# A list-ordered attention and mixer kernel: longer planned durations for batch 2's turned tiles, and a new order of its 1026 steps

## The chip, the cores and the metric

The kernel runs on one core of a Trainium2 chip. The metric is device time in microseconds (us); shown is the median of three runs of one build. Five engines work side by side, each through its own list of instructions in order: TensorE (PE, matmuls), VectorE (DVE), ScalarE (ACT), GpSimd (POOL) and SyncE (SP, which here only issues transfers). They wait for one another through semaphores.

## The reference

Batch 4, 8 heads, sequence 768, head size 48. The first half is a gated linear recurrence, the second an MLP mixer over its output:

```python
f = 1.0 / (1.0 + np.exp(-f_logit))
for t in range(S):
    state = f[:, :, t, :, None] * state + np.einsum('bhd,bhe->bhde', k[:, :, t], v[:, :, t])
    y[:, :, t] = np.einsum('bhd,bhde->bhe', q[:, :, t], state)
...
xt = x.transpose(0, 2, 1)
h = np.maximum(xt @ w_tok1, 0.0) @ w_tok2
u = x + h.transpose(0, 2, 1)
h2 = np.maximum(u @ w_ch1, 0.0) @ w_ch2
return (u + h2)
```

## The kernel before

The recurrence is computed in chunks. For each batch b the sequence is cut in three parts (P = 0, 1, 2) of two chunks each. Per part, ACT makes the logarithm of the gate (`gates`); DVE adds neighbouring steps (`two`); PE forms running sums; DVE and ACT make the gate factors (`first`, `GG`); DVE multiplies them into q and k (`qk`); these are turned so that head size lies on the partitions (`qT`, `kT`); PE forms the scores; DVE masks them (`AmT`, four tiles a part, with some of batch 0's masked by ACT and POOL together); PE forms the output (`within`, line 661, and the share of the state, `before`, line 655). Each state is copied to bf16 (`state_bd`, called sbd below). The mixer of a batch then runs tok1 (line 709), tok2 (725), the turn of u (`uT`), ch1 (784, in two halves th of the sequence, twelve columns cc each) and ch2 (803), and stores the result.

Batches 0 and 1 turn q, k and u with PE transposes that DVE or ACT copy out of PSUM. Batches 2 and 3 do it by transfers that SP issues: `dma_start_transpose` at line 531 (q into `qJ`, then rearranged into `qT` by POOL or ACT; k straight into `kT`) and at line 755 (u into `uT`).

No engine's list is in program order. `add` collects 1026 steps (ops); each knows what it needs and makes, on which engines it may run, and a cost. The tuple `ORDER` is a list written out by hand or by a search: an entry `code` stands for op `code // 4` on the engine number `code % 4` of those the op allows. `Plan.best` walks `ORDER`, gives each op a planned start (the latest of its inputs, its engine's last op and its PSUM bank), and emits the ops sorted by planned start. On any one engine that is the order of `ORDER` itself. The planned times decide two more things: which PSUM bank an op gets, and, before 25.5 us of planned time only, how many idle matmuls (line 852) fill PE's planned gaps.

A cost `("fix", own, till, wire, late)` says that the engine is taken for `own` ns, that the result is there after `till` ns, that the wires are taken for `wire` ns, and that `late` is added when the wires are busy. The planned gaps and banks come from these; the hardware waits for semaphores, not for planned times.

To read the ops that the text names: op 61 and 62 are the `qk` products of batch 0, part 0 (line 523); 64 and 66 its kT and qT (550); 86 and 88 the bf16 copies of its output (695); 92 is `first` of part 1 (499); 101 and 103 are kT and qT of part 1; 118 and 119 its second state copy (644); 143, 146 and 147 are DVE's masks of part 2 (624); 149 the state's decay of part 2 (633) and 150, 151 the copies of it; 121 and 153 are `within` of parts 1 and 2 (680); 14, 15 and 19 build the mask (408 to 412).

Of the kernel before, what the change touches and what calls it, by code (L numbers as in the profile page):

```python
# [255 lines left out]
def kernel(  # L256
# [45 lines left out]
    qk = [st([128, 2, 2, H, 64], BF16, f"qk{i}") for i in range(NQ)]  # L302
    qT = [st([128, HP, 128, 2], BF16, f"qT{i}") for i in range(NQ)]
    kT = [st([128, 2, HP, 128], BF16, f"kT{i}") for i in range(NQ)]
    qJ = [st([128, 2, HP, 128], BF16, f"qJ{i}") for i in range(2)]
# [580 lines left out]
```

## Time and profile before

| | |
|---|---|
| median of 3 runs | 166.11 us (165.8 to 166.11) |
| the profiled execution: its time / its span | 167.62 us / 165.9 us |
| granted TensorE clock, mean | 0.997 |
| busy: PE, DVE, ACT, POOL | 158.6, 128.8, 106.9, 61.7 us |
| instructions | 4990 |

The rows of the trace give a start, a length, an engine, the line of the kernel, the tile written and read, a count, and in square brackets how long the engine was idle before and what ended that. In the table of windows each row is a stretch of time and the busy time of each engine in it, with the count of instructions in parentheses. Rows of the chain of waits give start, length and what ran.

### The profile page before, as it was taken

The page shows a single profiled execution, that of the slowest core. Times are in us where ns is not written, and L with a number is a line of the kernel's source. Part 1 is how long each engine was busy: PE and PEld are TensorE (multiplying, and loading weights), DVE is VectorE, ACT ScalarE, POOL GpSimd, SP SyncE. Part 2 cuts the span into 40 slices and gives each one's busy share as a digit, 9 for nine tenths or more (in the row PEclk, how much of TensorE's full clock was granted, in tenths as well). Part 3 has the DMA queues.
Part 4 walks back from the last instruction along what each step waited for, and adds up shares of the span by engine and source line. Part 5 has one row for each costly group of instructions (what it writes and reads, how often), then busy time and mean ns, then how long its engine had stood idle before and what let it go on. Part 6 is the DMA issues. An engine that isn't in the chain of part 4 may idle for free.

```text
span 165.9 us, 4990 instructions
## 1 busy us (share of the span) xinstructions
PE 158.6 (96%) x2052; PEld 101.4 (61%) x2052; DVE 128.8 (78%) x284; ACT 106.9 (64%) x231; POOL 61.7 (37%) x86
## 2 busy tenths in 40 slices
PE   7889997999999999999999999999999999999992
PEld 3356765566667766666666765665666665656661
DVE  6748997589999999998999999988599526704331
ACT  3869784797899999999948966384811511623300
POOL 7961799964776820001914514200322020000000
PEclk9999999999999999999999999999999999999998
DMA  4999999999999999457699990991900030690506
GB/s 123 219 177 171 201 210 232 168 206 227 219 225 222 225 242 142 81 98 115 133 224 128 119 155 0 106 213 50 209 19 4 0 59 16 175 325 17 177 31 206
DMA packets 68183, 24.34 MB, mean 147 GB/s; under 512 B 60896, under 2 KB 67296, under 8 KB 68160
## 3 DMA queue, kind: packets, MB, share of 16 engines
q0 software_dynamic: 41856, 13.77, 68.2%
q1 hardware_dynamic: 25776, 10.06, 28.9%
q8 instruction: 16, 0.26, 0.7%
q10 hardware_dynamic: 528, 0.20, 0.4%
q14 instruction: 7, 0.06, 0.1%
HBM read 25.17 MB, written 4.72 MB: 180 GB/s over the span
## 4 chain that ended last, share of the span: by engine, by line
PE 82%; DMA 5%; ACT 4%; DVE 4%; issue 1%; POOL 1%; DVEq 0%; ACTq 0%; POOLq 0%
PE ps L803 28%; PE ps L784 28%; DMA qk_sb<-in_q_dram 5%; PE ps L709 5%; PE ps L725 4%; PE ps L665 3%; PE ps L581 3%; PE ps L657 2%; PE ps L546 2%; PE ps L599 2%; PE ps L766 1%; PE ps L481 1%; ACT state_bd L434 1%; ACT x_nat L434 1%; DVE qk L448 1%
## 5 line engine op out<-in xcount | busy, mean ns | idle before, releaser
L803 PE MATMUL ps<-w_ch,zT 128*128 128x384 bf16 (+2 forms) x300 | 54.0, 320 | 0.0
L784 PE MATMUL ps<-uT,w_ch 128*128 128x384 bf16 x288 | 51.6, 326 | 0.0
L784 PEld LDWEIGHTS <-w_ch 128*128 128x128 bf16 x288 | 27.8, 98 | 17.6
L803 PEld LDWEIGHTS <-zT 128*128 128x128 bf16 x300 | 27.9, 98 | 17.1
L443 ACT ACTIVATE zT<-ps 128x384 bf16<-128x384 f32 x57 | 25.1, 493 | 16.3 <-PE ps L784 16.1
L624 DVE TENSOR_TENSOR AmT<-ps,mask 128x512 bf16<-128x512 f32 x44 | 28.6, 685 | 1.5 <-PE ps L581 1.2
L445 DVE TENSOR_SCALAR zT<-ps 128x384 bf16<-128x384 f32 x39 | 20.6, 553 | 10.0 <-PE ps L784 8.9
L814 DVE TENSOR_TENSOR x_nat<-x_nat,ps 128x384 f32<-128x384 f32 (+2 forms) x25 | 13.1, 534 | 10.5 <-PE ps L803 10.5
L438 POOL CAST state_bd<-state 48x192 bf16<-48x192 f32 x15 | 5.7, 377 | 28.6 <-DVE state L641 25.8
L448 DVE TENSOR_TENSOR qk<-qk_sb,GG 128x768 bf16<-128x768 bf16 x24 | 12.9, 563 | 1.3 <-DMA qk_sb<-in_q_dram 1.3
L502 ACT ACTIVATE GG<-ps 128x384 bf16<-128x384 f32 x24 | 11.2, 485 | 3.5 <-DVE first L499 2.8
L357 POOL DMA_DIRECT2D v_sb<-in_v_dram x12 | 10.7, 894 | 6.3 <-DMA w_ch<-in_moe_w_ch_dram 3.7
L434 ACT ACTIVATE x_bf<-ps 128x384 bf16<-128x384 f32 x15 | 6.9, 483 | 8.5 <-PE ps L657 8.2
L519 ACT ACTIVATE GG<-first 128x384 bf16<-128x384 f32 x24 | 11.7, 517 | 0.2
L741 DVE TENSOR_TENSOR x_nat<-x_nat,ps 128x384 f32<-128x384 f32 x21 | 10.6, 549 | 1.4 <-PE ps L725 1.2
L357 POOL DMA_DIRECT2D qk_sb<-in_k_dram x12 | 10.9, 905 | 1.6 <-POOLq L870 0.8
L434 ACT ACTIVATE u_bf<-x_nat 128x384 bf16<-128x384 f32 x12 | 5.8, 518 | 8.6 <-DVE x_nat L741 8.6
L357 POOL DMA_DIRECT2D qk_sb<-in_q_dram x12 | 10.8, 898 | 0.5 <-DMA qk_sb<-in_q_dram 0.3
L852 PE MATMUL ps<-steady 128*128 128x512 f32 (+1 forms) x20 | 9.8, 610 | 1.0 <-DVE steady L372 1.0
L438 POOL COPY qT<-qJ 128x1024 bf16<-128x1024 bf16 x3 | 3.4, 1149 | 18.8 <-ACT zT L443 18.7
L709 PE MATMUL ps<-x_bf,w_tok 128*128 128x384 bf16 x48 | 10.4, 327 | 0.0
L434 ACT ACTIVATE x_nat<-ps 128x384 f32<-128x384 f32 x20 | 9.3, 492 | 0.1
(87 smaller groups left out, 231.3 us busy)
## 6 DMA issues: line engine op xcount, KB each, us to landing
out_dram<-x_nat SPq DMA_DIRECT2D x23, 192.0 KB, 2.3
f_sb<-in_f_logit_dram POOLq DMA_DIRECT2D x9, 384.0 KB, 8.9
qk_sb<-in_k_dram POOLq DMA_DIRECT2D x12, 192.0 KB, 8.8
qk_sb<-in_q_dram POOLq DMA_DIRECT2D x12, 192.0 KB, 9.0
v_sb<-in_v_dram POOLq DMA_DIRECT2D x12, 192.0 KB, 8.9
w_ch<-in_moe_w_ch_dram POOLq DMA_DIRECT2D x2, 576.0 KB, 9.0
w_ch<-in_moe_w_ch_dram POOLq DMA_DIRECT2D x1, 1152.0 KB, 10.6
f_sb<-in_f_logit_dram SPq DMA_DIRECT2D x2, 384.0 KB, 5.8
```

The costliest lines, as they stand in the source:

```text
L357: lambda eng=eng, into=held(dst[i], P), of=runs(src, b, P): eng.dma_start(out=into, in_=of),
L434: nc.scalar.activation(out_, in_, AF.Copy, bias=0.0, scale=1.0)
L443: nc.scalar.activation(out_, in_, AF.Relu, bias=0.0, scale=1.0)
L445: nc.vector.tensor_scalar(out_, in_, 0.0, None, ALU.max)
L448: (nc.vector if op.engine == DVE else nc.gpsimd).tensor_tensor(out_, a, b_, what)
L502: add(ACT, r, lambda n=n: nc.scalar.activation(GG[i][:, 1, n], sview(), AF.Exp, bias=0.0, scale=2.0 * n - 1.0), need=["tables"] if b == 0 ...
L519: add(ACT, r, lambda n=n: nc.scalar.activation(GG[i][:, 0, n], first[i], AF.Exp, bias=0.0, scale=2.0 * n - 1.0), need=[("first", i)] + ([" ...
L624: add(DVE, r, lambda into=into, made=made, m4=m4: nc.vector.tensor_tensor(into, made(), m4, ALU.mult), need=masks, make=[("AmT", i, js, pa ...
L709: add(PE, rank("tok1", rt), lambda rt=rt, kt=kt, pm=pm: nc.tensor.matmul(banks[pm.at][:, 0:DM], lhsT=w_tok1[:, kt, rt * 128:(rt + 1) * 128 ...
L784: nc.tensor.matmul(banks[pm.at][:, 0:384], lhsT=w[:, kt, c0:c0 + 128], rhs=uT[:, th, :, kt, :], start=(kt == 0), stop=(kt == 2))
L803: nc.tensor.matmul(banks[pm.at][:, 0:n1 - n0], lhsT=zT[:, kt, tt * 128:(tt + 1) * 128], rhs=w_ch2[:, kt, n0:n1], start=(kt == 0), stop=(kt ...
L814: add(DVE, rank("ch2", tt), lambda un=un, pm=pm, n=n1 - n0: nc.vector.tensor_tensor(un, un, banks[pm.at][:, 0:n], ALU.add), make=[("x_nat" ...
```

## The change

Two planned durations become functions of the batch, and the order is another one. No op is added or removed; what an op computes stays the same, but an op may run on another of the engines it allows.

```diff
-                    need=[("qk", s, 0), ("qk", s, 1)], make=[("qkT", s, 1) if n else ("qJ", i)], kind=("fix", 1350, 3400, 2000, 3500))
+                    need=[("qk", s, 0), ("qk", s, 1)], make=[("qkT", s, 1) if n else ("qJ", i)], kind=("fix", 1350, 4200 if b == 2 else 3800, 2000, 3500))
...
-                make=[("uT", 3 * th + j, d) for j in range(3) for d in range(3)], kind=("fix", 1350, 3400, 2000, 3500))
+                make=[("uT", 3 * th + j, d) for j in range(3) for d in range(3)], kind=("fix", 1350, 5200 if b == 2 else 3500, 2000, 3500))
```

Of `ORDER` nearly every line changes. Its first lines, which hold the part of batch 0 that the prediction walks through:

```diff
 ORDER = (
-    0, 4, 12, 16, 24, 28, 32, 8, 20, 188, 192, 196, 36, 40, 44, 76, 68, 48, 52, 60, 208, 356, 212, 220, 64, 224,
-    236, 240, 228, 360, 364, 368, 248, 244, 216, 376, 232, 372, 380, 388, 260, 80, 84, 265, 384, 200, 88, 296,
-    252, 92, 96, 56, 300, 256, 72, 309, 304, 396, 392, 204, 312, 268, 272, 504, 408, 400, 276, 288, 404, 316,
-    292, 280, 413, 508, 512, 320, 324, 100, 104, 108, 416, 420, 516, 448, 428, 452, 536, 532, 524, 520, 461,
-    457, 544, 540, 112, 116, 120, 284, 124, 128, 132, 432, 136, 328, 332, 340, 440, 344, 464, 336, 468, 348,
-    352, 444, 140, 476, 472, 556, 561, 528, 436, 424, 548, 552, 704, 592, 676, 708, 680, 564, 568, 596, 576,
-    572, 584, 588, 580, 480, 484, 488, 600, 604, 608, 612, 616, 493, 497, 144, 148, 152, 501, 621, 624, 156,
+    0, 4, 12, 16, 8, 20, 24, 28, 32, 188, 192, 196, 36, 40, 44, 56, 48, 52, 208, 212, 220, 64, 68, 356, 228,
+    224, 236, 240, 216, 232, 360, 364, 372, 244, 72, 248, 80, 88, 252, 260, 368, 256, 296, 300, 264, 305, 92,
+    96, 84, 200, 388, 384, 376, 308, 204, 380, 396, 392, 60, 312, 268, 272, 280, 316, 504, 76, 288, 276, 292,
+    400, 408, 508, 405, 320, 324, 413, 100, 104, 108, 512, 448, 416, 420, 516, 452, 461, 457, 524, 520, 540,
+    436, 424, 428, 532, 536, 440, 464, 544, 112, 116, 120, 124, 128, 132, 136, 140, 284, 144, 328, 332, 336,
+    556, 432, 444, 148, 348, 340, 468, 561, 528, 477, 548, 473, 552, 480, 484, 564, 568, 353, 576, 492, 497,
+    152, 580, 346, 156, 592, 704, 488, 676, 680, 708, 572, 588, 584, 608, 612, 596, 604, 600, 500, 616, 712,
...
```

Read as ops: 66 goes from ACT (265) to DVE (264), 101 from DVE (404) to ACT (405), 118 and 119 from ACT (472, 476) to DVE (473, 477), 86 from POOL (344) to DVE (346). On DVE op 92 (368) comes behind 61 and 62 (244, 248) instead of before them, 15 and 19 (60, 76) come later, and 149 (596) goes behind the masks 143, 147 and 146 (572, 588, 584). On POOL the weight loads and batch 1's first two loads (128 to 140) come before op 71 (284). SP's list begins as before with ops 2, 5 and 21; further on, both turns of u of batch 2 change places (707 before 706), and stores change places with transposes.

96 rows, old and new, of the table ORDER are left out of this document.

## The prediction

> **What bounds the kernel now.** I read the page first, then the windows of the trace, the chain of waits, and the timelines of PE and DVE over the first 35 us.
>
> ```profile
> span 165.9 us, 4990 instructions
> PE 158.6 (96%) x2052; PEld 101.4 (61%) x2052; DVE 128.8 (78%) x284; ACT 106.9 (64%) x231; POOL 61.7 (37%) x86
> ```
>
> The windows tell where PE's missing 4% lies:
>
> ```profile
> 25.00:30.00 5.00, 4.01 (x99) 2.67 (x92) 3.38 (x6) 2.39 (x6) 4.62 (x6) 1.00 1.39 218
> ...
> 35.00:40.00 5.00, 5.00 (x33) 2.98 (x32) 4.48 (x11) 4.67 (x13) 1.29 (x2) 1.00 1.45 234
> 40.00:60.00 20.00, 20.00 (x345) 13.62 (x344) 19.86 (x40) 18.53 (x41) 14.40 (x17) 1.00 1.80 219
> 60.00:80.00 20.00, 20.00 (x264) 13.08 (x262) 19.23 (x43) 19.65 (x44) 2.00 (x3) 1.00 0.87 123
> ```
>
> The first figure after the comma is PE; the windows from 80 to 160 us are as full. From 35 us on PE never stops, at a granted clock of 1.00. A busy PE could still be a slow one, so the chain of waits is asked for the pace:
>
> ```profile
> 34.12 2.93 PE ps L784 x18
> ```
>
> and, far behind,
>
> ```profile
> 107.38 3.90 PE ps L784 x24
> ```
>
> 2.93 / 18 and 3.90 / 24 both give 0.163 us a matmul of 384 columns, early and late alike. So after some 34 us the kernel is a fixed amount of PE work, and the end moves only by how early the head hands over to it, by stalls that a new order brings, and by the last store. (The Trainium skill, Perfetto Trace Analysis, section Identifying the Most-Contended Engine, calls matmul busy time a poor measure of what is left. By that rule a better order could still win behind a full PE; the one pace at both places speaks against it, and such a gain gets no term.)
>
> The head on PE:
>
> ```profile
> 25.96 0.57 PE L665 MATMUL ps<-v_sb,AmT 64*128 64x48 bf16 x31
> 27.52 0.18 PE L665 MATMUL ps<-v_sb,AmT 64*128 64x48 bf16 x1 [0.99 <-issue]
> ...
> 28.07 0.58 PE L665 MATMUL ps<-v_sb,AmT 64*128 64x48 bf16 x32
> ...
> 30.41 2.11 PE L725 MATMUL ps<-h1T,w_tok 128*128 128x384 bf16 x12
> ```
>
> Op 121 (`within` of part 1) runs 31 of its 32 matmuls, stands 0.99 us for nothing that the profile shows, and ends; op 153 (`within` of part 2) starts at 28.07, tok2 at 30.41. Had there been no stall, op 153 would have waited for DVE's last masks, which end at 24.92 + 1.89 = 26.81:
>
> ```profile
> 10.85 1.03 DVE L448 TENSOR_TENSOR qk<-qk_sb,GG 128x768 bf16<-128x768 bf16 x2 [1.32 <-DMA qk_sb<-in_q_dram]
> ...
> 24.92 1.89 DVE L624 TENSOR_TENSOR AmT<-ps,mask 128x512 bf16<-128x512 f32 x3
> ```
>
> From q's landing to the end of those masks, by one window:
>
> ```profile
> 10.85:26.81 15.96, 14.36 (x320) 10.23 (x321) 14.10 (x30) 11.92 (x25) 10.37 (x13) 1.00 1.53 198
> ```
>
> DVE, the third figure after the comma, is busy for 14.10 of 15.96 us and idle for 1.86. It is the head's engine.
>
> **The change, part by part.**
>
> *The longer durations.* A planned duration emits nothing. It moves a bank or the order, and idle matmuls only before 25.5 planned us, where batch 2 has no turned tile yet. Is there a wait on turned tiles that a later plan could save? Their landing times, of u:
>
> ```profile
> L755 SPq DMA_TRANSPOSE uT<-u_bf x4: 1281/1296/1627, 102.7 to 141.4; - x4
> ...
> DMA to landing us min/median/max: 3.2/3.2/4.5
> ```
>
> and of kT:
>
> ```profile
> DMA to landing us min/median/max: 3.0/3.5/6.8
> ```
>
> Some exceed the old 3.4 us, but PE is full where they are used: no wait, so 0 us. The cover was thin once: the first turn of u starts at 102.7 and, at the longest landing, is there at 107.2; ch1 of batch 2 starts at 107.38 in the chain above. In the new PE list nine groups of ch1 on the other half come first, 27 x 0.163 = 4.4 us, and cover the turn that is issued last. The price if a cover fails is what it lacks, at most 6.8 - 3.5 = 3.3 us for a landing at its worst; I take 0.
>
> *The order behind the head.* PE's work there is the same: 0 us unless a wait arises (rival three). Behind the last matmul the same two sums on DVE stand before the last store. On SP the stores of other rows before it are in another order, all ready before PE ends: 0, at most one store's issue, 0.4 us.
>
> *The head.* Before op 152, where part 2's output starts, PE's list holds the same 33 ops in both kernels, so what op 153 is shifted by, everything behind it is shifted by. On DVE, between 61 / 62 and the last of masks 143, 146, 147, ops come and go. By mean rows:
>
> ```profile
> L499 DVE TENSOR_TENSOR first<-ps,f_sb 128x384 f32<-128x384 f32 x12 | 6.6, 553 | 1.0 <-PE ps L486 1.0
> ...
> L436 DVE COPY kT<-ps 128x1024 bf16<-128x1024 bf16 x6 | 4.1, 686 | 0.1
> L436 DVE CAST x_bf<-ps 128x384 bf16<-128x384 f32 x6 | 3.3, 553 | 1.5 <-PE ps L657 1.4
> ...
> L436 DVE COPY qT<-ps 128x1024 bf16<-128x1024 bf16 x2 | 2.4, 1224 | 0.0
> ...
> L633 DVE TENSOR_TENSOR ps<-ps,glast 128x192 f32<-128x192 f32 x5 | 1.8, 363 | 1.3 <-PE ps L599 0.8 <-ACT glast L505 0.3 <-issue 0.2
> ...
> L436 DVE CAST state_bd<-ps 48x192 bf16<-48x192 f32 x3 | 1.1, 357 | 0.1
> ...
> L412 DVE COPY mask<-tri 64x64 bf16<-64x64 bf16 x2 | 0.7, 348 | 0.0
> L410 DVE TENSOR_TENSOR mask<-tri,ident 64x64 bf16<-64x64 bf16 x2 | 0.5, 228 | 0.0
> L408 DVE COPY mask<-tri 64x128 bf16<-64x128 bf16 x2 | 0.4, 216 | 0.0
> ```
>
> In come op 92, which ran while DVE waited for q and now stands behind it, 0.553; op 66, qT from ACT, 1.224; 118 and 119 from ACT, 2 x 0.357; 86 from POOL, 0.553 by its nearest row, which reads PSUM where op 86 reads SBUF; 19, 0.348; 15, 0.228: 3.62. Out go 101 (kT) 0.686, 149 0.363, 14 0.216: 1.27. The balance is 2.35. Rows of one engine overlap: three masks of 0.685 take 1.89, not 2.06, so 0.06 less each, 0.25 for the net four ops. That leaves 2.1 us more work on DVE.
>
> Against it stand the 1.86 us idle. In the new list DVE still waits for PE's turn of k in part 0 (about 0.1), for the first state product (0.2), and for part 2's turn of k (0.1): 0.45 with what lies between rows. So it eats 1.86 - 0.45 = 1.4, and the masks end 2.1 - 1.4 = 0.7 later, at 27.5. Bounds: 2.1 if it keeps every wait, 0 if the ops that ACT gave up shorten the remaining waits and DVE's queue packs closer. I take 0.7, from the waits whose causes stay. ACT's side: op 101 now stands ahead of 103 there, two copies of about 1 us in a row before part 1's scores, while DVE has part 0's three masks to do.
>
> In the old list PE still had op 122 and the state's share of op 153 to run after the masks (two times 0.17 us), in the new one op 122 lies earlier: -0.15. Against that, 149 and its copies 150, 151 now follow the masks:
>
> ```profile
> 26.06 0.67 ACT L434 ACTIVATE state_bd<-ps 48x192 bf16<-48x192 f32 x2 [0.47 <-PE ps L657]
> ```
>
> They take 0.36 + 0.67 us where op 153 itself gives 0.58 us of cover: `before(1)` of part 2 comes 0.45 late if nothing else is in the way, 0 if the copies of x_bf behind it set the pace. I take 0.25, the middle, for want of a row. Head: 0.7 - 0.15 + 0.25 = +0.8, against an old head without the stall, with bounds of -0.2 and +2.3.
>
> *The stall.* The profiled execution has 167.62 us with a span of 165.9; the median is 1.51 us lower, which leaves room for timed runs without the 0.99. I take the stall as the profiled execution's own. (The Trainium skill, Runtime: NRT & Kernel Launch, section Instruction fetch mechanics, has the refill of an engine's instructions mostly hidden; by that rule a stall without a releaser is no regular cost, and the sum stays. No row here shows a refill at 26.5 us.)
>
> **Sum.** Against the profiled execution: 167.62 - 0.99 + 0.8 = 167.4. For the median: 166.11 + 0 + 0 + 0.8 = 166.9 us.
>
> **Rivals.**
>
> *One, not slower: the stall is in every run and the change hides it.* It came at PE's 330th matmul of real work (idle ones left out). In the new list this lies at the end of part 2's first state product, where PE waits for masks anyway. Then the old median holds 0.99 that the new loses: 166.11 - 0.99 + 0.8 = 165.9. For it: the row names nothing that an order could move. Against: no second such stall on PE in 130 us, and the 1.51 us. It decides if the head's shift stays under 0.99.
>
> *Two, faster: that, and the added work fits DVE's waits.* 166.11 - 0.99 = 165.1. Against: 1.86 us of waits are less than 2.1 of work.
>
> *Three, slower still: DVE fails to keep up behind the head.* From 34 to 75 us it has next to no slack:
>
> ```profile
> 34.00:75.00 41.00, 41.00 (x555) 27.08 (x552) 40.27 (x84) 38.98 (x87) 16.69 (x20) 1.00 1.44 188
> ```
>
> 0.73 us idle in 41. Counted in the lists by mean rows, DVE's ops from the copies of batch 0's u to the masks of batch 2's first part are 96 (53.6 us) before and 99 (53.9) after. One op too late costs PE 0.55; 166.9 + 0.6 = 167.5, twice that at the worst. Against: the balance of both lists is within 0.3 us.
>
> **How the numbers follow.** Forecast 0.39, rival one 0.25, two 0.16, three 0.20. About 0.2%, 0.33 us, can be told from no change, so the band is 165.78 to 166.44. Below it lie rival two and 0.07 of rival one, 0.23; within it 0.15 of rival one and 0.03 of the forecast's own spread, 0.18; above it the rest, 0.59. The range of 165.3 to 167.9 leaves out most of rival two and the worse part of three; the forecast's own is 166.3 to 167.5.
>
> **What would show it.** Head right: DVE's timeline has a qT copy of 1.2 us before 15 us, the last three masks end near 27.5, tok2 starts near 30.2. Wrong: masks ended by 26.9. Rival one: no stall of 1 us on PE, and timed runs at 166 or less. Three: PE windows between 35 and 80 us that are not full, with DVE as releaser. PE waiting for a transposed tile would refute the zero for the durations.

## The result, and the profile after

| | before | changed |
|---|---|---|
| median of 4 runs | 166.0 us (165.8 to 166.11) | 168.2 us (167.53 to 169.04) |
| ratio to before, 95% interval | | 1.0136 (1.0088 to 1.0185) |
| the profiled execution: its time / its span | 167.62 / 165.9 us | 169.04 / 167.3 us |

The changed kernel is 2.2 us slower, where 0.8 was forecast, and the time lies above the range. Its page, the first two lines:

```profile
span 167.3 us, 5003 instructions
...
PE 159.3 (95%) x2054; PEld 101.9 (61%) x2054; DVE 130.4 (78%) x290; ACT 105.8 (63%) x225; POOL 63.2 (38%) x86
```

Behind the head PE is as full as before. The window from 35 to 155 us:

```profile
35.00:155.00 120.00, 120.00 (x1560) 76.80 (x1557) 102.11 (x215) 81.56 (x178) 36.04 (x51) 1.00 0.86 132
```

So the time was lost in the head. PE's timeline of the changed kernel at the place that the prediction walks through:

```profile
26.63 0.25 PE L657 MATMUL ps<-state_bd,qT 128*128 128x96 bf16 x2
28.03 0.24 PE L657 MATMUL ps<-state_bd,qT 128*128 128x96 bf16 x2 [1.15 <-issue]
...
29.08 0.58 PE L665 MATMUL ps<-v_sb,AmT 64*128 64x48 bf16 x32
...
31.48 2.11 PE L725 MATMUL ps<-h1T,w_tok 128*128 128x384 bf16 x12 [0.26 <-ACT h1T L443]
```

and DVE's:

```profile
10.35 0.56 DVE L448 TENSOR_TENSOR qk<-qk_sb,GG 128x768 bf16<-128x768 bf16 x1 [1.51 <-DMA qk_sb<-in_q_dram]
...
13.56 1.21 DVE L436 COPY qT<-ps 128x1024 bf16<-128x1024 bf16 x1
...
25.80 1.88 DVE L624 TENSOR_TENSOR AmT<-ps,mask 128x512 bf16<-128x512 f32 x3 [0.32 <-PE ps L581]
27.60 0.35 DVE L633 TENSOR_TENSOR ps<-ps,glast 128x192 f32<-128x192 f32 x1
```

The masks end at 27.68, as forecast (27.5), but tok2 starts at 31.48 and not at 30.2. And PE's stall for nothing that the profile shows is there again, 1.15 us long, one op further on, inside op 122.

A second trace of the kernel before, taken later (run e5 below: 166.29 us, span 164.6), is nearer to its median than the first. Its rows for the same places, PE's timeline first:

```profile
24.91 0.57 PE L665 MATMUL ps<-v_sb,AmT 64*128 64x48 bf16 x31
25.93 0.18 PE L665 MATMUL ps<-v_sb,AmT 64*128 64x48 bf16 x1 [0.45 <-issue]
26.04 0.52 PE L657 MATMUL ps<-state_bd,qT 128*128 128x96 bf16 x8
26.49 0.58 PE L665 MATMUL ps<-v_sb,AmT 64*128 64x48 bf16 x32
...
28.82 2.11 PE L725 MATMUL ps<-h1T,w_tok 128*128 128x384 bf16 x12
```

then DVE's:

```profile
9.55 1.02 DVE L448 TENSOR_TENSOR qk<-qk_sb,GG 128x768 bf16<-128x768 bf16 x2
...
23.87 1.89 DVE L624 TENSOR_TENSOR AmT<-ps,mask 128x512 bf16<-128x512 f32 x3
```

q's first product starts at 9.55 us here and at 10.85 in the first trace, where it waits for q's load; over all traces of this case it starts at 8.6 to 10.85. So head times are compared from that product on. From it to tok2 the kernel before takes 28.82 - 9.55 = 19.27 us, the changed one 31.48 - 10.35 = 21.13: 1.86 more. From tok2 to the end of the span both take the same, 164.6 - 28.82 = 135.8 and 167.3 - 31.48 = 135.8. The whole difference between these two traces is the head and q's landing. The 1.86 comes from one pair of traces; with the same head, the runs e1 and e2 below take 21.45 and 21.47 us from q to tok2, 2.2 more than the kernel before.

### The profile page after: what moved, and what is told of

Same layout as the page of the kernel before. It is cut to its first block, busy times and chain, and to the rows that moved or that the text cites. A ratio compares the mean times of both kernels' runs of the same rounds, so it can differ in the third digit from the quotient of the medians.

```text
span 167.3 us, 5003 instructions
## 1 busy us (share of the span) xinstructions
PE 159.3 (95%) x2054; PEld 101.9 (61%) x2054; DVE 130.4 (78%) x290; ACT 105.8 (63%) x225; POOL 63.2 (38%) x86
## 4 chain that ended last, share of the span: by engine, by line
PE 90%; DVE 2%; DMA 2%; ACT 2%; issue 1%; DVEq 0%
PE ps L803 28%; PE ps L784 28%; PE ps L709 5%; PE ps L581 4%; PE ps L725 4%; PE ps L546 3%; PE ps L665 3%; PE ps L852 3%; PE ps L657 2%; PE ps L599 2%; DMA f_sb<-in_f_logit_dram 2%; PE ps L479 2%; PE ps L766 1%; PE ps L486 1%; PE ps L481 1%
## 5 line engine op out<-in xcount | busy, mean ns | idle before, releaser
L803 PE MATMUL ps<-w_ch,zT 128*128 128x384 bf16 (+2 forms) x300 | 52.5, 320 | 0.0
L443 ACT ACTIVATE zT<-ps 128x384 bf16<-128x384 f32 x59 | 26.4, 492 | 21.0 <-PE ps L784 20.9
L624 DVE TENSOR_TENSOR AmT<-ps,mask 128x512 bf16<-128x512 f32 x44 | 29.1, 683 | 1.0 <-PE ps L581 0.8
L445 DVE TENSOR_SCALAR zT<-ps 128x384 bf16<-128x384 f32 x37 | 19.1, 550 | 5.6 <-PE ps L784 5.4
L438 POOL CAST state_bd<-state 48x192 bf16<-48x192 f32 x18 | 6.8, 380 | 28.7 <-DVE state L641 24.5
L852 PE MATMUL ps<-steady 128*128 128x512 f32 (+1 forms) x22 | 11.2, 620 | 1.0 <-DVE steady L372 1.0
L438 POOL COPY qT<-qJ 128x1024 bf16<-128x1024 bf16 x5 | 5.7, 1149 | 15.7 <-ACT GG L502 9.6
L434 ACT ACTIVATE u_bf<-x_nat 128x384 bf16<-128x384 f32 x15 | 7.3, 515 | 5.5 <-DVE x_nat L741 5.4
L725 PE MATMUL ps<-h1T,w_tok 128*128 128x384 bf16 x48 | 9.3, 326 | 0.3 <-ACT h1T L443 0.3
```

Of the source, the lines that this page charges most:

```text
L434: nc.scalar.activation(out_, in_, AF.Copy, bias=0.0, scale=1.0)
L443: nc.scalar.activation(out_, in_, AF.Relu, bias=0.0, scale=1.0)
L445: nc.vector.tensor_scalar(out_, in_, 0.0, None, ALU.max)
L624: add(DVE, r, lambda into=into, made=made, m4=m4: nc.vector.tensor_tensor(into, made(), m4, ALU.mult), need=masks, make=[("AmT", i, js, pa ...
L725: nc.tensor.matmul(banks[pm.at][:, 0:DM], lhsT=w_tok2[:, kt, tt * 128:(tt + 1) * 128], rhs=h1T[:, kt, :], start=(kt == 0 and not held), st ...
L803: nc.tensor.matmul(banks[pm.at][:, 0:n1 - n0], lhsT=zT[:, kt, tt * 128:(tt + 1) * 128], rhs=w_ch2[:, kt, n0:n1], start=(kt == 0), stop=(kt ...
```

## The stall, and what moves with it

Counting PE's matmuls, weight loads and the few instructions of its sequencer together in order of start, from 0 ("records"), the stall stands at record 703 to 705 in the first trace of before, in the second and in the changed kernel, though the op there is another. The page lists DMA queues, and two of them are called instruction. This is the larger one in the changed kernel:

```profile
q8 instruction: 16, 0.26, 0.6%
```

It has 16 packets and 0.26 MB in all, so 16 KB each. PE has 2 x 2054 matmuls and weight loads and 9 instructions of its sequencer, 4117 records; 4117 / 16 = 257 a packet. If a packet holds 256, the places like 704 are 256 apart: 192, 448, 704. The following table is worked out from the starts of the trace's records (us): q's first product; PE's record 192; start and landing of the first such packet, A; PE going on at record 448 (behind the wait there, where one lies within a few records); the second packet, B; PE going on at record 704; tok2; and tok2 less q.

```
                           q   r192  packet A      r448  packet B      r704   tok2  tok2-q
before, first trace     10.85 15.45 19.05-20.03   21.22 25.06-26.02   27.52  30.41  19.56
before, e5               9.55 14.40 17.80-18.73   20.17 23.59-24.57   25.93  28.82  19.27
changed                 10.35 16.31 19.62-20.59   21.92 25.59-26.55   28.03  31.48  21.13
e2, new head alone       9.25 15.20 18.83-19.77   21.20 24.84-25.82   27.26  30.72  21.47
e12, before, 12 units    9.30 15.03 18.54-19.47   20.99 25.18-26.15   27.61  30.64  21.34
e8, before, 20 cut       9.39 14.04 17.64-18.57   19.87 23.58-24.55   25.95  29.15  19.76
e10, before, 40 cut      9.34 11.66 14.71-15.68   18.45 21.75-22.71   24.22  28.17  18.83
e11, changed, 40 cut     8.60 11.46 14.37-15.27   18.93 22.19-23.09   24.53  29.25  20.65
```

In all 17 traces of this case packet B starts 3.1 to 4.2 us behind PE's record 448, and PE never goes on at record 704 before 1.23 us after B has landed; from 448 to 704 it takes 5.4 to 6.6 us, whatever the ops between are. Later in the kernel, with matmuls of 384 columns, PE takes 6.5 us and more for most stretches of 256 records, and no such stall shows.

The theory is then this. PE's list comes in packets of 256 records, each asked for when PE enters the one before. The head's small matmuls use a packet up as fast as the next one comes, so that what makes PE late at record 192 or 448 makes it late at 704 too, and what DVE does between these two places has no say. (The runs bear out the first half; e10 and e11 limit the second.) The rival is the prediction's picture: PE runs whenever its data is there, DVE's list sets the head, and the stall is a disturbance.

## The experiments

Where an experiment's ORDER takes one line less, its line numbers are one lower than those of before (L664 is L665 there); cut idle matmuls shift line 852 to 853 and 856. Ratios are to the kernel before, with 95% intervals, five rounds each if nothing else is said.

**e1, the order under the old durations.**

```diff
-                    need=[("qk", s, 0), ("qk", s, 1)], make=[("qkT", s, 1) if n else ("qJ", i)], kind=("fix", 1350, 4200 if b == 2 else 3800, 2000, 3500))
+                    need=[("qk", s, 0), ("qk", s, 1)], make=[("qkT", s, 1) if n else ("qJ", i)], kind=("fix", 1350, 3400, 2000, 3500))
...
-                make=[("uT", 3 * th + j, d) for j in range(3) for d in range(3)], kind=("fix", 1350, 5200 if b == 2 else 3500, 2000, 3500))
+                make=[("uT", 3 * th + j, d) for j in range(3) for d in range(3)], kind=("fix", 1350, 3400, 2000, 3500))
```

> The new order under the old planned durations of the turned tiles. Theory (the order does everything, the durations emit nothing): the same as the changed kernel, 168.2 us, ratio to before about 1.013. Rival (the durations move the PSUM banks of batch 2 and cost there): part of the 2.2 us is gone, below 167.5.

Measured: 1.0125 (1.0101 to 1.0149), 168.19 us. The order does it all; the durations emit nothing that costs.

**e2 and e3, head and rest apart.** The 198 ops of the head from one order, all others from the other. e2 (new head, old rest) and e3 (old head, new rest), each shown against the changed kernel at the place where the two are joined or at the list's begin:

```diff
     756, 772, 856, 872, 844, 828, 836, 793,
-    760, 744, 1192, 849, 833, 1012, 1016, 841, 980, 1036, 996, 1060,
+    1192, 849, 833, 972, 976, 744, 776, 840, 1212, 1216, 980, 1036,
```

```diff
-    0, 4, 12, 16, 8, 20, 24, 28, 32, 188, 192, 196,
+    0, 4, 12, 16, 24, 28, 32, 8, 20, 188, 192, 196,
...
-    760, 744, 1192, 849, 833, 1012, 1016, 841, 980, 1036, 996, 1060,
+    1188, 1192, 849, 833, 824, 760, 744, 1012, 1016, 841, 980, 1036,
```

> The new order for the 198 steps of the head (all that PE does up to the first ch1 of batch 0), the old order for the rest. Theory (head): the new head hands over 2.0 us later than the old one does when the old one has no stall of 0.99 us on PE, and the stall is in the profiled execution alone: tok2 starts at 31.5 us, and the time is 168.0, nearly all of the 2.2 us. Rival one (the stall is in every run; the head costs about 1.0, the rest the other 1.2): 167.0. Rival two (the rest does it all): 166.0 to 166.3.

> The old order for the 198 steps of the head, the new order for the rest. Theory (head): 166.0 to 166.3, what the tail adds. Rival one (the stall is in every run): 167.2. Rival two (the rest does it all): 168.2.

Measured: e2 1.0105 (1.0077 to 1.0134), so 0.0105 x 166.07 = 1.7 us; e3 1.0073 (1.0049 to 1.0097), 1.2 us. The head alone brings most of the loss. But e3 was expected at 166.0 to 166.3 and missed: behind the old head, which hands over earlier, the new rest costs 1.2 us that it does not cost behind the new head. Its trace shows where. PE in e3, from 35 to 155 us, and one wait in it:

```profile
35.00:155.00 120.00, 119.74 (x1551) 76.18 (x1549) 99.90 (x209) 78.90 (x173) 36.08 (x51) 1.00 0.87 132
```

```profile
42.64 0.32 PE L481 MATMUL ps<-two_lo,tri 128*128 128x384 bf16 x1 [0.26 <-DVE two_lo L469]
...
151.60 10.59 PE L802 MATMUL ps<-w_ch,zT 128*128 128x384 bf16 x76
```

The same last row in the changed kernel:

```profile
153.35 10.59 PE L803 MATMUL ps<-w_ch,zT 128*128 128x384 bf16 x76
```

e3's tok2 starts at 28.65, 2.83 ahead of the changed kernel's 31.48; its last ch2 group is only 1.75 ahead. It gave 1.1 us back while the window shows 0.26 idle. A row of a 384-column matmul is 0.33 us long while the next one starts 0.163 later, so a busy window hides waits of up to 0.16 us each. Matmul by matmul, the lead is 2.56 us at the 49th of ch1 (41.53 against 44.09) and 1.88 at the first of ch2 (44.10 against 45.98): 0.7 of the 1.1 us goes around the one wait above. The chain of waits leads from it back to a load:

```profile
28.41 11.25 DMA f_sb<-in_f_logit_dram
...
39.68 0.85 ACT f_sb L456
...
41.43 0.57 DVE two L447
...
42.03 0.57 DVE two_lo L469
...
42.64 0.32 PE ps L481
```

So this is not rival three's mechanism. DVE waited as well (0.33 us, for ACT), and ACT for the gate's load, which landed at 39.66; in the changed kernel the same step of ACT starts without a wait:

```profile
41.53 0.87 ACT L457 ACTIVATE f_sb<-f_sb 128x768 f32<-128x768 f32 x1
```

Where the other 0.4 us went is not shown.

**e4, one part of the late head undone**: the state product of part 2 ahead of the scores, its decay and copies ahead of the masks.

```diff
-    484, 564, 568, 353, 576, 492, 497,
+    484, 592, 564, 568, 596, 353, 576, 604, 600, 492, 497,
-    152, 580, 346, 156, 592, 704, 488, 676, 680, 708, 572, 588, 584, 608, 612, 596, 604, 600,
+    152, 580, 346, 156, 704, 488, 676, 680, 708, 572, 588, 584, 608, 612,
```

> The changed kernel with one part of its head undone: PE's state product of part 2 (op 148) ahead of the scores 141 and 142, the decay 149 ahead of DVE's masks and its copies 150 and 151 ahead of ACT's copies, as before. Theory (the decay behind the masks holds PE up from about 27.8 to 28.7, and the stall is not in timed runs): 0.6 to 1.0 faster than the changed kernel, about 167.3. Rival (the stall is in every run, and PE is behind it there anyway): no gain, 168.0 to 168.3; tok2 starts near 31.4 as in the changed kernel.

Measured: 1.0192 (1.0160 to 1.0223), 0.9 us slower than the changed kernel: neither theory had that. The stall stayed at its record, with other work around it:

```profile
26.92 0.33 PE L656 MATMUL ps<-state_bd,qT 128*128 128x96 bf16 x4 [1.07 <-issue]
...
28.49 0.57 PE L664 MATMUL ps<-v_sb,AmT 64*128 64x48 bf16 x32
```

From the stall's end to tok2 (30.90) lie 3.98 us here, 3.45 in the changed kernel: work had been moved to the far side of the record. That is half of the loss; the other half lies ahead of the stall's end, which comes 18.16 us behind q's first product instead of 17.68. This miss is what led to counting records.

**e5, the kernel before once more** (no edit, one execution).

> The kernel before, unchanged, for a second trace of it. In six traces so far PE goes on at its 704th recorded instruction (matmuls and weight loads together) 1.25 to 1.60 us behind the landing of a 16 KB packet of the instruction queue, which starts 5.7 to 6.3 us before that. Theory (refill: PE's list comes in packets, and the head is paced by them): again a stall there, of 0.4 to 1.0 us, ending 1.2 to 1.6 us behind the second such packet; span 164.2 to 164.9 us, and q's first product near 9.3 us instead of 10.85, which is what made the earlier trace 1.5 us longer than the median. Rival (that stall belonged to one execution): PE runs through that place.

Measured: 166.29 us, span 164.6, q's first product at 9.55, a stall of 0.45 us that ends 25.93 - 24.57 = 1.36 us behind packet B. As the theory said; the rows stand above. The 5.7 to 6.3 us in the text above are the time from record 448 to record 704; packet B itself starts 25.93 - 23.59 = 2.3 us before PE goes on.

**e6 and e7, the head in two pieces.** The first 72 ops (to the scores of part 0, the turns of part 1 and the sums of part 2) from one order, the other 126 of the head from the other, old rest; idle matmuls given by hand as in the kernel that each piece is from. e6 (new late piece), then e7 (new early piece), against the kernel before, at the joint:

```diff
-    408, 400, 276, 288, 404, 316, 292, 280, 413, 508, 512, 320, 324, 100, 104, 108,
+    408, 400, 276, 288, 316, 292, 280, 508, 405, 320, 324, 413, 100, 104, 108, 512,
...
-KEPT = 3
+KEPT, FILLS = 3, {53: 13, 65: 4, 78: 8, 104: 1, 116: 2, 139: 4, 176: 1, 152: 1}
...
-            if e == PE and free[PE] < until and t - free[PE] > 270:
-                n = int(t / 410) if not free[PE] else int((t - free[PE] - 50) / 215)
+            if e == PE and code // 4 in FILLS:
+                n = FILLS[code // 4]
```

```diff
-    408, 400, 276, 288, 404, 316, 292, 280, 413, 508, 512, 320, 324, 100, 104, 108,
+    504, 76, 288, 276, 292, 400, 408, 508, 404, 413, 512, 320, 324, 100, 104, 108,
...
-KEPT = 3
+KEPT, FILLS = 3, {53: 13, 90: 4, 78: 12, 116: 3, 139: 1, 120: 3}
```

> The old order for the first 72 steps of the head (to the scores of part 0, the turns of part 1 and the sums of part 2), the new one for the other 126 of its 198 steps, the old order for the rest; idle matmuls as in the kernel that each piece is from. Theory (refill: the new head loses about 1.2 us before PE's 192nd record, where the first packet is asked for, and 0.6 us behind the 704th, nothing between them): about 166.6. Rival (data: what DVE does between the two, with op 149 behind the masks, sets the end): 167.4 or more.

> The reverse of the run before: the new order for the first 72 steps, the old one for the rest of the head and of the kernel. Theory (refill): about 167.3, 1.2 us behind the kernel before. Rival (data): 166.4 or less, since the late part of the head is the old one.

Measured: e6 1.0037 (1.0013 to 1.0062), 0.6 us; e7 1.0066 (1.0031 to 1.0100), 1.1 us. Both as the packet theory said, and together e2's 1.7. Most of the head's loss arises in those first 72 ops and the idle matmuls among them.

**e8, 34 more records ahead of the head**, in the time when PE has only idle matmuls:

```diff
-        for one in [steady32] * (n // 4) + [steady] * (n % 4):
+        cut = 5 if n == 13 else 0
+        for _ in range(4 * cut):
+            nc.tensor.matmul(banks[NBANK - 1][:, :128], lhsT=steady.broadcast_to((128, 128)), rhs=steady.broadcast_to((128, 128)), start=True, stop=True)
+        n -= cut
+        for one in [steady32] * (n // 4) + [steady] * (n % 4):
```

> The kernel before with one edit: of its first 13 planned units of idle matmuls five are cut into 20 matmuls of 128 columns, the same columns but about 34 more instructions in PE's list ahead of the head, at a time when PE has nothing else. Theory (refill): the packets are asked for 34 records earlier in the real work, the first one some 2.5 us earlier; the stall in op 121 is gone, and the time falls by 0.3 to 0.6 us, to 165.5 to 165.8. Rival (the packets don't pace the head): 166.0 to 166.2, with the stall where it was in the real work or not at all.

Measured: 1.0067 (1.0040 to 1.0094), 1.1 us slower. Half of that goes with the clock: five of the twelve executions had a mean granted clock of 0.99 and took 167.5 to 168.0 us, while the other seven, at 1.0, have a median of 166.57, 0.5 above the kernel before. The trace (166.86 us, 1.0) shows 0.5 as well, 19.76 against 19.27 at tok2. The sign was wrong, and by the theory's own rule it should have been foreseen. The table shows record 192 at 14.04, only 0.4 us earlier than in e5: it still lies in the burst that starts with the scores of part 0. Packet A came at nearly the same time (17.64 and 17.80), while record 448 lay in earlier work, inside op 83:

```profile
18.51 0.64 PE L665 MATMUL ps<-v_sb,AmT 64*128 64x48 bf16 x18
19.87 0.35 PE L665 MATMUL ps<-v_sb,AmT 64*128 64x48 bf16 x14 [0.72 <-issue]
```

So the stall moved with the count of records, against the work: that speaks for packets. It called for an edit that carries record 192 over the idle matmuls at 12 us.

**e10 and e11, 70 more records**: the same edit with `cut = 10`, in the kernel before (e10) and in the changed one (e11).

```diff
-        cut = 5 if n == 13 else 0
+        cut = 10 if n == 13 else 0
```

> As the run with 20 cut matmuls, but with 40: some 70 records more ahead of the real work instead of 34. Theory (a packet is asked for when PE enters record 192, 448 and so on, and its instructions can run some 5.8 us later): 34 records left record 192 in the same burst of small matmuls and only moved record 448 to earlier work, so that PE waited longer; with 70, record 192 lies ahead of the idle matmuls of op 78, the first packet starts near 15.7 us instead of 17.7, both stalls are gone, and the time is 165.4 to 165.8, faster than before. Rival (each idle instruction more costs): over 167.3, slower than with 20.

> The changed kernel with the same 40 cut matmuls. Theory (packets): its stalls at records 448 and 704 shrink, 0.2 to 0.7 faster than the changed kernel, 167.5 to 168.0; the copies 150 and 151 behind the masks then hold op 153 until 28.7 us of the changed kernel's trace, so no more than that. Rival: no change or slower, 168.2 or more.

Measured: e10 0.9981 (0.9967 to 0.9994), 0.3 us faster than before by the ratio, 0.2 by the medians: the version that beats both kernels, if barely. e11 1.0069 (1.0042 to 1.0095), 167.24 us, 1.0 us faster than the changed kernel, more than expected. In e10 packet A starts 3 us earlier and op 121 runs through:

```profile
24.70 0.58 PE L665 MATMUL ps<-v_sb,AmT 64*128 64x48 bf16 x32
25.21 0.52 PE L657 MATMUL ps<-state_bd,qT 128*128 128x96 bf16 x8
25.65 0.58 PE L665 MATMUL ps<-v_sb,AmT 64*128 64x48 bf16 x32
```

20 cut matmuls cost 0.5 us at the same clock, 40 gain 0.3, with no other edit and no change in what DVE and ACT have to do. The rival has no place for that.

But the packets do not carry the whole loss. With the 40 cut matmuls in both kernels the change still costs 167.24 - 165.91 = 1.3 us, of 2.2, and DVE's masks of part 2 set where op 153 starts. In e10 and then in e11:

```profile
23.66 1.88 DVE L624 TENSOR_TENSOR AmT<-ps,mask 128x512 bf16<-128x512 f32 x3
```

```profile
25.06 1.29 DVE L624 TENSOR_TENSOR AmT<-ps,mask 128x512 bf16<-128x512 f32 x2 [0.22 <-PE ps L581]
...
26.65 0.57 PE L665 MATMUL ps<-v_sb,AmT 64*128 64x48 bf16 x32
```

The masks end at 25.54 and 26.35, 16.20 and 17.75 us behind q's first product, and `within` of part 2 starts 0.11 and 0.30 behind them. (In e11 0.98 of the 17.75 is a wait of DVE for ACT's gate factors right behind q, which had landed early, at 8.60.)

**e9 and e12, the idle matmuls ahead of op 78** (the second state product of part 0). The new order's plan puts 12 units there, the old one's 8. e9: the changed kernel with 8; e12: the kernel before with 12.

```diff
-KEPT = 3
+KEPT, FILLS = 3, {53: 13, 90: 4, 78: 8, 104: 1, 116: 2, 139: 4, 176: 1, 152: 1}
```

```diff
-KEPT = 3
+KEPT, FILLS = 3, {53: 13, 65: 4, 78: 12, 116: 3, 139: 1, 120: 3}
```

> The changed kernel with one number other: 8 planned units of idle matmuls ahead of op 78 (PE's second state product of part 0) instead of 12, as many as before had. Theory (idle matmuls: the later planned time of op 78 brings four more units, 0.9 us on PE, of which its data would cover half): 0.4 to 0.9 faster than the changed kernel, 167.3 to 167.8. Rival (DVE's longer list before that place sets it): no change, 168.1 to 168.3.

> The kernel before with that one number alone: 12 units ahead of op 78 instead of 8. Theory (idle matmuls, and the packets behind them paced from there): 0.9 us slower, about 167.0, most of what the new early head costs alone (1.1). Rival (PE has slack there, DVE sets the head): 166.1 to 166.3.

Measured: e12 1.0050 (1.0034 to 1.0066), 0.8 us, as expected; e9 1.0145 (1.0107 to 1.0183), no gain, a miss. In e12 four units more, just ahead of op 78, cost 0.8 us in the median. Its trace is of an execution 1.0 us above that median (167.87 us), so its sizes are not typical, but it shows the two waits at the two records:

```profile
11.95 2.80 PE L852 MATMUL ps<-steady 128*128 128x512 f32 x6
...
20.99 0.59 PE L852 MATMUL ps<-steady 128*128 128x512 bf16 x2 [1.28 <-issue]
...
27.61 0.20 PE L665 MATMUL ps<-v_sb,AmT 64*128 64x48 bf16 x3 [1.11 <-issue]
```

In e9 the time was not there to be had, since op 78's data comes late too. (From 27.67 us on PE's granted clock in this trace is 0.50 for 3.41 us; only rows ahead of that are read. The other five executions, without such a stretch by their mean clock, have a median of 168.56.)

```profile
15.35 0.34 PE L599 MATMUL ps<-v_sb,qk 64*64 64x48 bf16 x11 [0.66 <-ACT state_bd L434]
```

That is 5.7 us behind q's first product (9.63 in e9); in e5 PE starts op 78 at 14.04, 4.5 us behind it.

**e13, e14 and e15: what makes op 78's data late?** e13: op 66 (qT) back on ACT in the changed kernel, with 8 units. e14: op 66 on DVE in the kernel before. e15: e13 with ACT's queue ahead of the state copy 77 as before.

```diff
-    256, 296, 300, 264, 305, 92,
+    256, 296, 300, 265, 305, 92,
```

```diff
-    236, 240, 228, 360, 364, 368, 248, 244, 216, 376, 232, 372, 380, 388, 260, 80, 84, 265, 384, 200, 88, 296,
+    236, 240, 228, 360, 364, 368, 248, 244, 216, 376, 232, 372, 380, 388, 260, 80, 84, 264, 384, 200, 88, 296,
```

```diff
-    300, 264, 305, 92, 96, 84, 200, 388, 384, 376, 308, 204, 380,
+    300, 388, 265, 305, 308, 92, 96, 84, 384, 376, 200, 204, 380,
```

> The changed kernel with op 66 (qT of part 0) back on ACT, and 8 units of idle matmuls ahead of op 78 as before had (without that they would cover the gain). Theory (the qT copy of 1.2 us on DVE stands ahead of the state copies 76 and 77, op 78 waits for these, and the packets of PE's list are paced from there): op 78 starts some 4.7 us behind q's first product instead of 5.6 to 5.7, and the time is 0.7 to 1.1 lower than the changed kernel's, 167.1 to 167.5. Rival (several small edits on DVE, none of them alone): under 0.3 gained, 167.9 or more.

> The kernel before with op 66 alone on DVE, idle matmuls as before. Theory: op 78 waits for the state copies until some 5.6 us behind q's first product, PE waits over 1 us at its 448th and 704th record as in the run with the longer idle group, and the time is 0.7 to 1.1 higher than before, 166.8 to 167.2. Rival: 166.1 to 166.4.

> The changed kernel with ACT's queue in front of the state copy 77 as before: op 66 (qT) back on ACT, 77 right behind it, the gate steps 96, 94 and 50 behind 77, 97 ahead of 66; 8 units of idle matmuls ahead of op 78. (With 66 alone moved, ACT stood in the way: 77 came 5.6 us behind q's first product, behind two gate products, a copy and a step of part 2's gate.) Theory (what stands ahead of the state copies, on whichever engine, makes the early head late, and the packets keep it late): op 78 starts 4.4 to 4.8 us behind q's first product instead of 5.6 to 5.9, and the time falls by 0.6 to 1.0 from the changed kernel's, to 167.2 to 167.6. Rival (the early head's cost lies elsewhere): 168.0 or more.

Measured: e14 1.0034 (1.0005 to 1.0064), 0.6 us: in the old order the qT copy on DVE alone costs about half of what the early head costs, less than expected; op 78 starts 5.1 us behind q's first product, not 5.6. e13 1.0156 (1.0112 to 1.0199) gained nothing (median 168.57; 168.33 over the four executions at a mean clock near 1.0, against the changed kernel's 168.2), and e15 1.0190 (1.0161 to 1.0219), 169.02 us, lost 0.8 us more. Both missed their forecasts. PE's rows show the next wait each time, e13 first, then e15:

```profile
15.06 0.34 PE L598 MATMUL ps<-v_sb,qk 64*64 64x48 bf16 x11 [1.12 <-ACT state_bd L433]
...
21.77 0.62 PE L598 MATMUL ps<-v_sb,qk 64*64 64x48 bf16 x16 [1.14 <-DVE state_bd L435]
```

```profile
13.74 0.34 PE L598 MATMUL ps<-v_sb,qk 64*64 64x48 bf16 x10
...
16.37 0.61 PE L545 MATMUL ps<-ident,qk 128*128 128x128 bf16 x8 [0.69 <-ACT glast L504]
...
21.64 0.43 PE L598 MATMUL ps<-v_sb,qk 64*64 64x48 bf16 x16 [1.08 <-DVE state_bd L435]
```

With qT on ACT, the state copy stood behind gate steps there, and op 78 starts 5.9 us behind q's first product in e13; with these behind it (e15, op 78 at 13.74, 5.0 us behind q's first product), they came late for part 1's turn, and the next state copy held PE at 21.64. In the new early head several chains are equally late, and no single edit of it carries the 1.1 us. Which ones together do is left open.

## Why the prediction was wrong, step by step

- **The sign, and the place** were right: slower, and in the head. The durations cost nothing (e1), and no PE row waits for a turned tile.
- **The stall failed as a step.** "I take the stall as the profiled execution's own": it is in the typical execution too (e5, 0.45 us), at the same record. What was the first trace's own was q's late landing, 10.85 - 9.55 = 1.3 us of the 1.51 that I had read as room for timed runs without a stall. Rival one rested on the right half, a stall fixed to a place in PE's list; but the change does not hide it, it makes it longer, 1.15 us. With the records shifted in both kernels the change costs 1.3 us instead of 2.2 (e10, e11), so by these medians some 0.9 of the loss hangs on where the stalls stand. I had counted 330 matmuls of real work and not asked what else counts instructions. The Trainium skill, Runtime: NRT & Kernel Launch, section Instruction fetch mechanics, has the block size (16 KiB, 256 instructions), which these traces confirm, and calls the crossing mostly hidden. In this head it is not: 0.45 to 1.15 us at record 704 in the rows above. I had quoted its second half and passed over the first.
- **"So it eats 1.86 - 0.45 = 1.4, and the masks end 2.1 - 1.4 = 0.7 later"** is the term of the sum that was mis-sized. Of DVE from q's first product to the end of part 2's masks, the windows are, in e5 and in the changed kernel:

```profile
9.55:25.76 16.21, 14.95 (x324) 10.72 (x326) 14.08 (x31) 13.30 (x30) 10.54 (x14) 1.00 1.59 191
```

```profile
10.35:27.68 17.33, 15.14 (x324) 10.58 (x324) 15.68 (x34) 13.51 (x27) 12.54 (x14) 1.00 1.53 203
```

  DVE has 15.68 - 14.08 = 1.6 us more work (forecast 2.1), but its idle time falls only from 2.13 to 1.65, by 0.5 (forecast 1.4). The masks end 17.33 - 16.21 = 1.1 later, not 0.7. The waits that stay are for PE: 0.25 us for the turn of k and 0.12 and 0.39 for the state products of part 0, then 0.21 for part 2's turn and 0.32 for its scores, where 0.45 in all had been forecast. Part 2's turn had itself stood for DVE's product:

```profile
23.27 0.98 PEld L546 LDWEIGHTS <-qk 128*128 128x128 bf16 x16 [0.57 <-DVE qk L448]
```

  A wait whose cause moves along with DVE's own list is not eaten by more work in that list. That the masks ended at 27.68, near the 27.5 of the forecast, was chance: q had landed half a microsecond earlier than in the trace that the sum started from.
- **"-0.15" and "I take 0.25, the middle"**, what lies between the masks and op 153, was +0.7: 26.49 - 25.76 = 0.73 in e5, 29.08 - 27.68 = 1.40 changed. PE comes from its stall at 28.03 and has 0.8 us of other work before op 153, whose share of the state starts at 28.81 and whose `within` at 29.08. The copies 150 and 151 behind the masks end at 27.99 + 0.66 = 28.65, but by the kernel's line 682 only `before(1)`, behind op 153, reads them, and it follows at 29.59 without a wait. ACT's row:

```profile
27.99 0.66 ACT L434 ACTIVATE state_bd<-ps 48x192 bf16<-48x192 f32 x2 [0.63 <-DVE ps L633]
```

  In e10 and e11, where no stall reaches past the end of the masks, this stretch is 0.11 and 0.30 us, so +0.2 for the new order: that is near the forecast's +0.1, and the rest of the +0.7 goes with the stall.

  The sum as it was: 1.1 + 0.7 + 0.1 (op 153 to tok2, 2.33 and 2.40) = 1.9 us from q to tok2, against a forecast of 0.8.
- **"The order behind the head: 0"** held in the changed kernel (tok2 to the end of the span 135.8 in both), and the tail's 0 with it, but the late head covered something: behind the old head the new rest costs 1.2 us (e3), most of it around a wait that leads back to a gate's load. "PE is full" was argued from windows, which do not show waits under 0.16 us.

## What to carry to other kernels

A wait on PE that has no releaser deserves a count of PE's instructions up to it: if it stands at the same count in two kernels with different work there, it belongs to the list and not to the execution, and edits should be judged by what they put ahead of and behind that place. Where an engine's idle time is to absorb new work, ask of each wait what ends it, and whether the new work delays that too. Take head times from the first data that lands, not from the start of the span.

## What the runs showed of the hardware

PE goes on at record 704 of its list no earlier than 1.23 us after a 16 KB packet of the instruction queue has landed (17 traces), and that packet starts 3.1 to 4.2 us behind record 448. With matmuls as small as this head's (32 of them in 0.58 us) PE is faster than that. The regularity is measured, and in e8 and e10 the stall moved with the count; that PE's entry into a packet is what asks for the next one is inferred from it. What fills the 3 to 4 us was not tried. One thing goes with it: in the two traces of before and in the changed kernel's, a packet starts 2.7 to 5.0 us behind records 192, 448 and 704, while POOL's loads keep the DMA engines full, and between 2.4 us ahead of and 1.4 us behind the corresponding records past 105 us, where these loads are over. PE's matmuls there are longer too, so this does not say which of the two matters. Idle matmuls count as instructions too: some 34 records more of them cost 0.5 us at the same clock, 70 gained 0.3.

In two traces, e9 and e13, PE's granted clock is 0.50 for 3.41 us in the middle of the head, from the end of a wait of PE of 1.07 us in e9 and around the end of one of 1.14 us in e13. The windows, e9 first:

```profile
27.67:31.08 3.41, 3.41 (x46) 2.14 (x46) 0.56 (x1) 1.30 (x4) 3.41 (x5) 0.50 1.92 184
```

```profile
21.60:25.01 3.41, 3.24 (x54) 2.11 (x54) 3.23 (x8) 2.66 (x6) 2.68 (x3) 0.50 1.16 211
```

In the changed kernel's trace a wait of 1.15 us is followed by no such stretch, so what brings it on is open.
